# Hash attention with a gated MLP: stripes of hash results with gaps, gated rows kept in PSUM, and the last output row in three column parts

## The chip, the core and the metric

The kernel runs on one core of a Trainium2 chip. [...] VectorE (DVE), ScalarE (ACT) and GpSimd (POOL) do the elementwise work, and SyncE (SP) issues most transfers. The time is the device time of one execution in microseconds; the comparison is by the median of several executions.

## The reference

Attention over hash buckets, and behind it a gated feed-forward network with a gated residual. Sizes: 4 batches, 8 heads, 768 positions, 64 values per head; 3072 tokens of 512 values; a hidden width of 1536. All inputs are fp32.

```python
q_bits = (einsum('bhsd,dk->bhsk', q, proj) > 0)          # 6 sign bits per position
k_bits = (einsum('bhsd,dk->bhsk', k, proj) > 0)
mask   = bucket(q_bits)[:, :, :, None] == bucket(k_bits)[:, :, None, :]
scores = where(mask, (q @ k.T) / sqrt(64), -1e9)
attn   = exp(scores - max(scores)); attn /= attn.sum(-1) + 1e-9
x      = (attn @ v), as 3072 x 512
out    = x + sigmoid(x @ w_res) * ((gelu(x @ w_gate) * (x @ w_val)) @ w_out)
```

## The kernel before

The 32 heads are taken as 16 pairs, four pairs to a batch. For every pair, q and k are loaded in fp32 (`load`), cast to bf16 into one of four buffers `nat` (`cast`, POOL), and extended by six columns that hold the hash bits as plus or minus one half, so that one product of 71 rows gives score and bucket comparison together. The extended rows are turned so that the feature runs over the partitions: in the first batch by PE (`turn_pe`, copied to `aug` by `turned` on DVE, L329), later by a transposing DMA (`turn`, L308, issued by SP).

The hash bits come about in four steps. `tr` (L240, DVE) transposes the loaded tile in blocks of 32 x 32; `hash_mm` (L251, PE) multiplies by the projection into a PSUM tile `hs`; `hash_tok` (L266, DVE) transposes this back into a tile of 12 stripes of 32 columns, which is the SBUF tile `ht` for pairs 1, 2 and 3 and the PSUM tile `htp` for all later pairs; `bits` (L282) compares with zero and writes the six columns, in four instructions of 32 partitions by 12 rows by 6 values. For the first batch's q all four are DVE's, for its k POOL and DVE take turns. Pair 0 has its own path (`hash_one`, `bits_one`).

Each pair has nine chunks. `scores` (L448, PE) fills a PSUM tile of 128 x 1024 (`sp`, two of them), ACT takes the exponential (L459), `values` (L421, PE) multiplies by v into accumulators `av`, and `finish` divides (L372 and L373, DVE). POOL prepares v: `vals_a` (L338) and `vals_s` (L346 to L350). In the first batch the order of all steps is written out by hand in the list `ORDER`; each engine runs its instructions in that order. The weights of the network are loaded by POOL in twelve pieces (`w0` to `w11` in the lists, L193).

When a batch's attention is done, `gate_val` (L472 PE, L489 ACT, L492 DVE) computes the hidden layer in twelve blocks; beside the first batch's blocks stand the steps of the list `BESIDE` (loads, hashes and turns of the next pairs). Then `project` gives the output rows, six of 128 tokens per batch: four products `rps` for the residual gate (L504) with a tanh on ACT (L508), twelve products `fps` (L518), and on DVE two operations, L521 (gate plus one, times the product) and L524 (one half of that, plus x). SP sends the row out (L526). In the first three batches these products are spread over the next batch's chunks, and `rps` and `fps` alternate between two PSUM banks; the last batch's six rows run one behind the other at the end, with `fps` in the two `sp` tiles.

The function `project` splits the very last row by columns:

```python
for k0, k1 in ((0, 3), (3, 4)) if last else ((0, KM),):
    cs = slice(k0 * P, k1 * P)
```

Of the kernel before, what the change touches and what calls it, by code (L numbers as in the profile page):

```python
# [9 lines left out]
FP32 = mybir.dt.float32  # L10
# [36 lines left out]
def kernel(  # L47
# [12 lines left out]
    nc = tc.nc  # L60
    B, H, S, D = q.shape
    NBITS = proj.shape[1]
    DMODEL = H * D
    DFF = moe_w_gate.shape[1]
    P = 128
    KM = DMODEL // P
# [4 lines left out]
    HT = 2 * T  # L71
# [22 lines left out]
    sm_pool = ctx.enter_context(tc.tile_pool(name="sm", bufs=2))  # L94
    sc_ps = ctx.enter_context(tc.tile_pool(name="sc_ps", bufs=2, space=PSUM))
    av_ps = ctx.enter_context(tc.tile_pool(name="av_ps", bufs=2, space=PSUM))
# [5 lines left out]
    x_tok, x_sb = {}, {}  # L102
# [79 lines left out]
    for s in range(NS):  # L182
        cs = bass.ts(s, DFF // NS)
# [3 lines left out]
    for s in range(3):  # L187
        n = KF // 3
# [8 lines left out]
    def nat_of(x):  # L197
        return nat[(2 * x[0] + x[1]) % NN]
# [13 lines left out]
    t32, hsum, htok = {}, {}, {}  # L212
    free_banks, held_banks = ["r", "f"], {}

    def take(what=None):
        tag = free_banks.pop(0)
        if what is None:
            free_banks.append(tag)
        else:
            held_banks[what] = tag  # L220
        return tag

    def give(what):
        if what in held_banks:
            free_banks.append(held_banks.pop(what))
# [31 lines left out]
    def ht_of(jobs):  # L257
        return jobs[0]

    def hash_tok(jobs, psum=False):  # L260
        n = 32 * len(jobs)
        if psum:
            ht = mm_ps.tile([P, HT, 32], FP32, tag=take(("ht", ht_of(jobs))), name="htp")
        else:
            ht = sm_pool.tile([P, HT, 32], FP32, tag="ht", name="ht")
        nc.vector.transpose(ht[:n].rearrange("p c n -> p (c n)"),  # L266
                            hsum[jobs[0]][:n].rearrange("p c n -> p (c n)"))
        give(jobs[0])
        for j, x in enumerate(jobs):
            htok[x] = (ht, j)  # L270
        ht_left[id(ht)] = (len(jobs), ("ht", ht_of(jobs)))

    def bits(p, side, engs=(nc.vector,)):
        x = (p, side)
        ht, j = htok.pop(x)
        n, what = ht_left.pop(id(ht))
        if n > 1:
            ht_left[id(ht)] = (n - 1, what)
        else:
            give(what)  # L280
        for a in range(4):
            engs[a % len(engs)].tensor_scalar(  # L282
                nat_of(x)[32 * a:32 * a + 32, :, D:D + NBITS],
                ht[32 * j:32 * j + 32, :, NBITS * a:NBITS * (a + 1)], 0.0, 0.5,
                op0=ALU.is_gt, op1=ALU.subtract)


# [73 lines left out]
    av = {}  # L361
# [136 lines left out]
    def project(b):  # L498
        hh = hidden[b]
        for t in range(T):  # L500
            last = b == B - 1 and t == T - 1
            rps = mm_ps.tile([P, DMODEL], FP32, tag=take(), name="rps")
            for kk in range(KM):
                nc.tensor.matmul(rps, x_sb[b][:, kk, t, :], wr[:, kk, :],  # L504
                                 start=(kk == 0), stop=(kk == KM - 1))
                if kk == KM - 1:
                    th = g_pool.tile([P, DMODEL], FP32, tag="th", name="th")
                    nc.scalar.activation(th, rps, AF.Tanh, scale=0.5)  # L508
                yield
            o = o_pool.tile([P, DMODEL], FP32, tag="o", name="o")  # L510
            for k0, k1 in ((0, 3), (3, 4)) if last else ((0, KM),):
                cs = slice(k0 * P, k1 * P)
                if b < B - 1:
                    fps = mm_ps.tile([P, DMODEL], FP32, tag=take(), name="fps")
                else:
                    fps = sc_ps.tile([P, DMODEL], FP32, tag="sp", name="fps")
                for m in range(KF):
                    nc.tensor.matmul(fps[:, cs], hh[:, m, bass.ts(t, P)], wo[:, m, cs],  # L518
                                     start=(m == 0), stop=(m == KF - 1))
                    yield  # L520
                nc.vector.scalar_tensor_tensor(o[:, cs], th[:, cs], 1.0, fps[:, cs],  # L521
                                               op0=ALU.add, op1=ALU.mult)
                o3 = o[:, cs].rearrange("p (k n) -> p k n", n=P)
                nc.vector.scalar_tensor_tensor(o3, o3, 0.5, x_tok[b][:, k0:k1, t, :],  # L524
                                               op0=ALU.mult, op1=ALU.add)
                nc.sync.dma_start(out_t[b, t][:, cs], o[:, cs])  # L526

# [63 lines left out]
    def tokens(ps, psum=False):  # L591
        hash_tok([(p, side) for p in ps for side in range(2)], psum)
# [6 lines left out]
    def hash_pe(ps, s, bits_at):  # L599
        jobs = [(p, side) for p in ps for side in range(2)]  # L600
        for i in range(4):
            pe(s + i // 2 - 1, lambda i=i: hash_mm(jobs, (i % 2,), (i // 2,)))
        at(s, lambda: tokens(ps))
        for p, s in zip(ps, bits_at):
            at(s, lambda p=p: bits(p, 0), lambda p=p: bits(p, 1, (nc.gpsimd, nc.vector)))
# [30 lines left out]
    for p in range(1, 2 * HP):  # L636
        for side in range(2):
            job(f"tr{p}{side}", lambda p=p, side=side: tr(p, side))
            job(f"cs{p}{side}", lambda p=p, side=side: cast(p, side, nc.gpsimd))
            job(f"bt{p}{side}", lambda p=p, side=side: bits(p, side, (nc.vector,) if side == 0 or p >= HP else (nc.gpsimd, nc.vector)))  # L640
            job(f"tu{p}{side}", lambda p=p, side=side: turn(p, side))
            for hi in range(2):
                job(f"tp{p}{side}{hi}", lambda p=p, side=side, hi=hi: turn_pe(p, side, hi))
                job(f"td{p}{side}{hi}", lambda p=p, side=side, hi=hi: turned(p, side, hi, nc.vector))
# [21 lines left out]
    def lay(b, m, x):  # L666
        gv(b, m, lambda: bits(*x), lambda: turn(*x))
# [45 lines left out]

    gate_val(0, begun)
    mlp.append(project(0))
    for s in range(NSLOT, LAST):
        p, c = divmod(s, NCH)
        b, slot = divmod(s, NSLOT)
        cur = scores(p, c)
        for piece in side_pe.pop(s, []):  # L720
            piece()
        mlp_mm(AHEAD + (slot + 1) * (NMM - HELD - AHEAD) // NSLOT - done[0])
        pending.append(cur)
        while len(pending) > LAG:
            values(*pending.pop(0))
        for piece in side_work.pop(s, []):
            piece()
        if slot == NSLOT - 1:
            values(*pending.pop(0))
            ps = (HP * (b + 1), HP * (b + 1) + 1)  # L730
            mlp_mm(4)
            flush()
            begun = [gv_mm(b, 0, w, 0, KM - 1) for w in (wg, wv)]
            if b < B - 1:
                mlp_mm(NMM)
                gate_val(b, begun, lambda: hashed(ps))
            else:
                x_turn(b, HP - 1)
                mlp_mm(HELD - 7)
                gv(b, 0, lambda: mlp_mm(NMM))  # L740
                gate_val(b, begun, lambda: mlp_mm(3))
            done[0] = 0
            mlp.append(project(b))
# [33 lines left out]
```

## Time and profile before

| | |
|---|---|
| median of 3 executions | 346.66 us (346.12 to 347.13) |
| profiled execution | 346.07 us, its span 344.4 us |
| PE | 333.5 us busy, 97% of the span |
| ACT | 206.2 us, 60% |
| DVE | 191.7 us, 56% |
| POOL | 85.6 us, 25% |
| moved by DMA | 42.90 MB |

The profile is one execution. A row of a timeline gives start, length, engine, line, operation, tiles, shapes and count; behind it, in square brackets, stands how long the engine was idle before it and what ended that. Rows of neighbouring instructions of one kind are merged, so a row with x2 covers two instructions and what lies between them. A group row gives minimum, median and maximum of one instruction in ns.

### The profile page before, as it was taken

The page shows a single profiled execution, that of the slowest core. Times are in us where ns is not written, and L with a number is a line of the kernel's source. Part 1 is how long each engine was busy: PE and PEld are TensorE (multiplying, and loading weights), DVE is VectorE, ACT ScalarE, POOL GpSimd, SP SyncE. Part 2 cuts the span into 40 slices and gives each one's busy share as a digit, 9 for nine tenths or more (in the row PEclk, how much of TensorE's full clock was granted, in tenths as well). Part 3 has the DMA queues.
Part 4 walks back from the last instruction along what each step waited for, and adds up shares of the span by engine and source line. Part 5 has one row for each costly group of instructions (what it writes and reads, how often), then busy time and mean ns, then how long its engine had stood idle before and what let it go on. Part 6 is the DMA issues. An engine that isn't in the chain of part 4 may idle for free.

```text
span 344.4 us, 7546 instructions
## 1 busy us (share of the span) xinstructions
PE 333.5 (97%) x3064; PEld 204.3 (59%) x3112; DVE 191.7 (56%) x404; ACT 206.2 (60%) x232; POOL 85.6 (25%) x162
## 2 busy tenths in 40 slices
PE   8998999999999999999999999999999999999994
PEld 4675766555666655655666665656566665566442
DVE  6979737656344856757344784747244444343333
ACT  3888972226999962224999982223999984223110
POOL 3887920317055000260043200242030000000000
PEclk9999999999999999999999999999999999999999
DMA  7959998999976743528366642725430220000022
GB/s 215 376 128 280 146 241 149 181 127 176 189 175 188 210 107 78 101 39 148 82 194 188 227 115 65 131 49 109 75 100 32 55 55 30 33 0 0 32 79 75
DMA packets 71171, 42.90 MB, mean 125 GB/s; under 512 B 49504, under 2 KB 68192, under 8 KB 71136
## 3 DMA queue, kind: packets, MB, share of 16 engines
q1 hardware_dynamic: 64720, 37.17, 44.0%
q0 software_dynamic: 6336, 5.24, 10.2%
q8 instruction: 24, 0.39, 0.5%
q14 instruction: 11, 0.09, 0.1%
q10 hardware_dynamic: 80, 0.00, 0.0%
HBM read 29.36 MB, written 6.29 MB: 104 GB/s over the span
## 4 chain that ended last, share of the span: by engine, by line
PE 90%; DVE 3%; ACT 3%; issue 1%; DMA 1%; SPq 0%; POOL 0%; DVEq 0%; ACTq 0%; POOLq 0%
PE sp L472 34%; PE fps L518 18%; PE sp L448 17%; PE av L421 9%; PE rps L504 6%; PE hs L251 3%; ACT hh L459 2%; DMA ld<-in_k_dram 1%; PE pt L320 1%; PE wps L174 1%; DVE nat L282 1%; PE hs L293 1%; DVE aug L329 1%; ACT gt L489 0%; SPq L308 0%
## 5 line engine op out<-in xcount | busy, mean ns | idle before, releaser
L459 ACT ACTIVATE e<-sp 128x1024 bf16<-128x1024 f32 x108 | 109.0, 1028 | 8.0 <-PE sp L448 2.8
L489 ACT ACTIVATE gt<-sp 128x768 bf16<-128x768 f32 x48 | 38.9, 810 | 92.8 <-PE sp L472 92.8
L448 PE MATMUL sp<-aug,aug 71*128 71x256 bf16 (+1 forms) x384 | 85.8, 325 | 2.0 <-DVE aug L329 1.6
L518 PE MATMUL fps<-wo,hh 128*128 128x512 bf16 (+2 forms) x275 | 74.6, 369 | 1.4
L492 DVE TENSOR_TENSOR hh<-gt,sp 128x768 bf16<-128x768 bf16 x48 | 45.7, 953 | 48.0 <-PE sp L472 43.9
L472 PE MATMUL sp<-x_sb,wv 128*128 128x256 bf16 (+1 forms) x378 | 70.6, 325 | 0.7 <-DVE hh L492 0.4
L472 PE MATMUL sp<-x_sb,wg 128*128 128x256 bf16 (+1 forms) x373 | 70.4, 324 | 0.7
L421 PEld LDWEIGHTS <-e 128*128 128x128 bf16 x864 | 40.2, 97 | 25.1
L472 PEld LDWEIGHTS <-wv 128*128 128x128 bf16 x384 | 37.6, 98 | 25.3 <-issue 0.6
L472 PEld LDWEIGHTS <-wg 128*128 128x128 bf16 x384 | 36.7, 98 | 26.0 <-issue 2.3
L421 PE MATMUL av<-va,e 128*128 128x65 bf16 x864 | 43.4, 193 | 0.0
L518 PEld LDWEIGHTS <-hh 128*128 128x128 bf16 x300 | 27.4, 97 | 22.5
L459 ACT ACTIVATE hh<-sp 128x1024 bf16<-128x1024 f32 x36 | 34.4, 1026 | 5.1 <-PE sp L448 5.0
L521 DVE SCALAR_TENSOR_TENSOR o<-th,fps 128x512 f32<-128x512 f32 (+2 forms) x25 | 16.7, 666 | 36.9 <-PE fps L518 30.0
L448 PEld LDWEIGHTS <-aug 71*128 71x128 bf16 x384 | 29.2, 97 | 13.0 <-issue 2.0
L346 POOL TENSOR_TENSOR v<-ldv 128x384 f32<-128x384 f32 x16 | 16.0, 999 | 64.1 <-DMA ldv<-in_v_dram 64.0
L240 DVE STREAM_TRANSPOSE t<-ld 128x768 f32<-128x768 f32 (+1 forms) x34 | 30.5, 912 | 1.6 <-DMA ld<-in_k_dram 1.4
L400 DVE COPY av<-av 128x390 f32<-128x390 f32 x24 | 13.6, 567 | 29.7 <-PE av L396 29.7
L208 POOL TENSOR_SCALAR nat<-ld 128x768 bf16<-128x768 f32 (+1 forms) x16 | 13.8, 860 | 60.1 <-DMA aug<-nat 55.4
L504 PE MATMUL rps<-wr,x_sb 128*128 128x512 bf16 x90 | 25.6, 378 | 0.3
L508 ACT ACTIVATE th<-rps 128x512 f32<-128x512 f32 x24 | 14.3, 594 | 18.5 <-PE rps L504 18.5
L210 POOL CAST nat<-ld 128x768 bf16<-128x768 f32 (+1 forms) x17 | 13.3, 783 | 39.7 <-DMA aug<-nat 38.8
(64 smaller groups left out, 242.5 us busy)
## 6 DMA issues: line engine op xcount, KB each, us to landing
ldv<-in_v_dram SPq DMA_DIRECT2D x16, 384.0 KB, 5.4
out_dram<-o SPq DMA_DIRECT2D x23, 256.0 KB, 2.0
ld<-in_q_dram SPq DMA_DIRECT2D x15, 384.0 KB, 5.6
ld<-in_k_dram SPq DMA_DIRECT2D x15, 384.0 KB, 5.2
wg<-in_moe_w_gate_dram POOLq DMA_DIRECT2D x4, 384.0 KB, 8.5
wv<-in_moe_w_val_dram POOLq DMA_DIRECT2D x4, 384.0 KB, 9.0
wo<-in_moe_w_out_dram POOLq DMA_DIRECT2D x3, 512.0 KB, 9.4
wr<-in_moe_w_res_dram POOLq DMA_DIRECT2D x1, 512.0 KB, 7.7
```

The costliest lines, as they stand in the source:

```text
L240: nc.vector.transpose(t32[p, side][:, sl].rearrange("p c h n -> p (c h n)"), raw[p, side][:, sl].rearrange("p c d -> p (c d)"))
L346: nc.gpsimd.tensor_add(v3, vs[:, :, 0:3, :], vs[:, :, 3:6, :])
L421: nc.tensor.matmul(av[p, hi][:, qt, :], e[:, off:off + P], va[:, hi, jt, 0:D + 1], start=first, stop=(p >= HP and jt == T - 1), skip_group ...
L448: nc.tensor.matmul(sp[:, off:off + nq * P], ks[0:KA, hi * T + jt, :], qs[0:KA, hi * T + qt0:hi * T + qt0 + nq, :], start=True, stop=True)
L459: nc.scalar.activation(e, sp, AF.Exp, scale=float(ALPHA))
L472: nc.tensor.matmul(sp[:, c0:c1], w[:, kk, bass.ts(m, P)], xs[:, kk, c0:c1], start=(kk == 0), stop=(kk == KM - 1))
L489: nc.scalar.activation(gt, sp[:, 0:S], AF.Gelu)
L492: nc.vector.tensor_mul(hidden[b][:, m, :], gt, ps[1][:, 0:S])
L504: nc.tensor.matmul(rps, x_sb[b][:, kk, t, :], wr[:, kk, :], start=(kk == 0), stop=(kk == KM - 1))
L508: nc.scalar.activation(th, rps, AF.Tanh, scale=0.5)
L518: nc.tensor.matmul(fps[:, cs], hh[:, m, bass.ts(t, P)], wo[:, m, cs], start=(m == 0), stop=(m == KF - 1))
L521: nc.vector.scalar_tensor_tensor(o[:, cs], th[:, cs], 1.0, fps[:, cs], op0=ALU.add, op1=ALU.mult)
```

## The change

Three edits. First, the SBUF tile `ht` gets 15 stripes in place of 12, and the results are written and read as three groups of four with an empty stripe behind each; the PSUM tile `htp` keeps its 12. The instructions and their order stay, only their access patterns differ. Second, L521 writes its result over the product in its PSUM bank, in place of the SBUF tile `o`, and L524 reads it from there and writes `o`. Third, the last row has three column parts of 256, 128 and 128 columns in place of two of 384 and 128, the last of them in a bank of the pool that held the attention's accumulators; this adds twelve products with their weight loads, two DVE operations and one output transfer.

```diff
+    def stripes(ht):
+        n = ht.shape[1]
+        return ht.rearrange("p (a c) n -> p a c n", a=3)[:, :, 0:HT // 3] if n > HT else \
+            ht.rearrange("p (a c) n -> p a c n", a=3)
+
     def hash_tok(jobs, psum=False):
...
-            ht = sm_pool.tile([P, HT, 32], FP32, tag="ht", name="ht")
-        nc.vector.transpose(ht[:n].rearrange("p c n -> p (c n)"),
-                            hsum[jobs[0]][:n].rearrange("p c n -> p (c n)"))
+            ht = sm_pool.tile([P, HT + 3, 32], FP32, tag="ht", name="ht")
+        nc.vector.transpose(stripes(ht[:n]).rearrange("p a c n -> p a (c n)"),
+                            hsum[jobs[0]][:n].rearrange("p (a c) n -> p a (c n)", a=3))
...
             engs[a % len(engs)].tensor_scalar(
-                nat_of(x)[32 * a:32 * a + 32, :, D:D + NBITS],
-                ht[32 * j:32 * j + 32, :, NBITS * a:NBITS * (a + 1)], 0.0, 0.5,
+                nat_of(x)[32 * a:32 * a + 32, :, D:D + NBITS].rearrange("p (a c) n -> p a c n", a=3),
+                stripes(ht[32 * j:32 * j + 32, :, NBITS * a:NBITS * (a + 1)]), 0.0, 0.5,
                 op0=ALU.is_gt, op1=ALU.subtract)
...
-            for k0, k1 in ((0, 3), (3, 4)) if last else ((0, KM),):
+            for k0, k1 in ((0, 2), (2, 3), (3, 4)) if last else ((0, KM),):
                 cs = slice(k0 * P, k1 * P)
-                if b < B - 1:
+                if last and k1 == KM:
+                    fps = av_ps.tile([P, DMODEL], FP32, tag="av", name="fps")
+                elif b < B - 1:
...
-                nc.vector.scalar_tensor_tensor(o[:, cs], th[:, cs], 1.0, fps[:, cs],
+                nc.vector.scalar_tensor_tensor(fps[:, cs], th[:, cs], 1.0, fps[:, cs],
                                                op0=ALU.add, op1=ALU.mult)
                 o3 = o[:, cs].rearrange("p (k n) -> p k n", n=P)
-                nc.vector.scalar_tensor_tensor(o3, o3, 0.5, x_tok[b][:, k0:k1, t, :],
+                g3 = fps[:, cs].rearrange("p (k n) -> p k n", n=P)
+                nc.vector.scalar_tensor_tensor(o3, g3, 0.5, x_tok[b][:, k0:k1, t, :],
                                                op0=ALU.mult, op1=ALU.add)
```

## The prediction

> **What bounds the kernel now.** I read the page first (busy shares, chain), then the stage table, then the engines' timelines wherever an engine that should be full had a hole.
>
> ```profile
> PE 333.5 (97%) x3064; PEld 204.3 (59%) x3112; DVE 191.7 (56%) x404; ACT 206.2 (60%) x232; POOL 85.6 (25%) x162
> PE 90%; DVE 3%; ACT 3%; issue 1%; DMA 1%; SPq 0%; POOL 0%; DVEq 0%; ACTq 0%; POOLq 0%
> ```
>
> PE is busy for 97% of the span and carries 90% of the chain. The change leaves PE's columns as they are, so it can only win where PE stands still. One such place lies in the first batch, another is the tail behind the last product. The stage table (length; then busy us with counts of PE, PEld, DVE, ACT, POOL; clock; DMA share; GB/s) shows the first:
>
> ```profile
> 28.00:33.30 5.30, 3.87 (x50) 2.58 (x48) 5.14 (x11) 4.41 (x5) 5.13 (x10) 1.00 1.01 269
> 33.30:46.90 13.60, 13.37 (x209) 10.12 (x210) 9.81 (x18) 13.12 (x14) 11.56 (x19) 1.00 1.28 191
> 46.90:83.00 36.10, 35.34 (x268) 21.06 (x272) 22.64 (x53) 12.46 (x17) 10.32 (x16) 1.00 1.02 158
> ```
>
> From 28.0 to 33.3 us DVE is busy for 5.14 of 5.30 and PE for only 3.87. PE and ACT are nearly full afterwards. The timelines of PE, ACT and DVE around it:
>
> ```profile
> 31.72 0.38 PE L448 MATMUL sp<-aug,aug 71*128 71x256 bf16 x2
> 33.30 0.39 PE L448 MATMUL sp<-aug,aug 71*128 71x512 bf16 x1 [1.20 <-DVE aug L329]
> ```
> ```profile
> 15.21 5.83 ACT L459 ACTIVATE hh<-sp 128x1024 bf16<-128x1024 f32 x6 [0.29 <-PE sp L448]
> 21.45 1.94 ACT L459 ACTIVATE hh<-sp 128x1024 bf16<-128x1024 f32 x2 [0.41 <-PE sp L448]
> 23.86 8.55 ACT L459 ACTIVATE hh<-sp 128x1024 bf16<-128x1024 f32 x9 [0.47 <-PE sp L448]
> 33.78 1.02 ACT L459 ACTIVATE hh<-sp 128x1024 bf16<-128x1024 f32 x1 [1.37 <-PE sp L448]
> ```
> ```profile
> 28.07 0.90 DVE L282 TENSOR_SCALAR nat<-ht 32x72 bf16<-32x72 f32 x2
> 28.99 0.98 DVE L240 STREAM_TRANSPOSE t<-ld 128x768 f32<-128x768 f32 x1
> 29.98 2.21 DVE L282 TENSOR_SCALAR nat<-ht 32x72 bf16<-32x72 f32 x4
> 32.22 1.02 DVE L329 COPY aug<-pt 71x768 bf16<-71x768 bf16 x2
> ```
>
> The reader should see one wait on three engines: PE cannot finish a score tile until two copies of turned operands are done (32.22 to 33.24), ACT waits 1.37 us for that tile, and the copies are late because six bit writes (L282) in front of them took 3.11 us. Elsewhere the same write is short:
>
> ```profile
> L282 DVE TENSOR_SCALAR nat<-htp x96: 214/228/239, 53.3 to 241.3; 32x72 bf16<-32x72 f32 x96
> L282 DVE TENSOR_SCALAR nat<-ht x18: 185/194/1061, 15.6 to 31.1; 32x72 bf16<-32x72 f32 x18
> L282 POOL TENSOR_SCALAR nat<-ht x6: 448/468/513, 15.7 to 25.7; 32x72 bf16<-32x72 f32 x6
> ```
>
> Read from PSUM (htp) it never takes over 239 ns; read from SBUF (ht) its median is shorter, 194, but it can take 1061. The long ones, one by one, and what POOL does then:
>
> ```profile
> 28.07 0.69 DVE L282 TENSOR_SCALAR nat<-ht 32x72 bf16<-32x72 f32 x1
> 31.13 1.06 DVE L282 TENSOR_SCALAR nat<-ht 32x72 bf16<-32x72 f32 x1
> ```
> ```profile
> 27.81 0.82 POOL L338 CAST va<-ldv 128x768 bf16<-128x768 f32 x1 [1.70 <-DMA ldv<-in_v_dram]
> ```
> ```profile
> 28.62 0.98 POOL L193 DMA_DIRECT2D wg<-in_moe_w_gate_dram  x1
> 29.60 0.75 POOL L193 DMA_DIRECT2D wv<-in_moe_w_val_dram  x1
> 30.34 0.75 POOL L193 DMA_DIRECT2D wg<-in_moe_w_gate_dram  x1
> 31.10 1.02 POOL L346 TENSOR_TENSOR v<-ldv 128x384 f32<-128x384 f32 x1
> ```
>
> The write of 28.07 ends at 28.76, just behind POOL's cast (28.63); that of 31.13 ends at 32.19, just behind POOL's sum (32.12). The transpose of 28.99 ran through POOL's next two instructions in 0.98 us. So it is this form of write, and not DVE as a whole, that POOL holds up.
>
> **The gaps in the hash results.** In the built program the bit write's source becomes 3 groups of 4 stripes, while its destination stays 12 rows of 6. [...] No row shows such a source, so the write lies between no gain (it is still held) and the PSUM row's 228 ns. I take 228, since that is the same operation in the form that is never held. [...]
>
> Six writes at 0.228 make 1.37 in place of 3.11 us: DVE is 1.74 us earlier and the copies end at 31.50 in place of 33.24. What is late next is PE itself: its first part of that tile starts at 31.72 and the rest would follow at about 32.1, so PE's hole of 1.20 closes and no more. ACT's earlier block ends at 23.86 + 8.55 = 32.41; the tile used to reach it 0.48 after PE's restart, which gives 32.4 to 32.6. **Gain 1.20**, between 0 and ACT's 1.37.
>
> The other twelve writes were not held, and grow by 0.034 each: six in a row, 0.2 us, at 15.58 and at 23.90. Behind both lie blocks in which ACT has six and nine tiles without a hole (the rows of 15.21 and 23.86), so PE is ahead there. Zero to 0.2 each; I take 0.05 in all. If that cover were gone it would be 0.4. The two transposes into the striped tile write the same 384 elements per partition: nothing. The six POOL writes also get the third level: shown only as 0.468 us without it. POOL's 768-element cast of 0.82 bounds them above (two in a row, 0.7 later, with ACT's block behind), and DVE's 0.228 below. I take no change.
>
> **What follows the hole.** A stage that starts 1.2 us earlier meets the DMA engines as they were; their share is 1.28 and then 1.02 in the table. One wait there is already for a load:
>
> ```profile
> 62.10 0.98 DVE L240 STREAM_TRANSPOSE t<-ld 128x768 f32<-128x768 f32 x1 [1.36 <-DMA ld<-in_k_dram]
> ```
>
> That load is issued by SP behind turned operands, which come from DVE and move with it, while POOL's weight loads hardly move since POOL is full (5.13 of 5.30). If the load keeps its place, all of the gain is given back; if it moves along, none. I take 0.15 lost.
>
> **Gated rows over their bank.** The second operation reads PSUM in place of a second SBUF tile, and the first writes PSUM. The tail has both kinds at equal sizes:
>
> ```profile
> 337.25 0.69 DVE L524 SCALAR_TENSOR_TENSOR o<-o,x_tok 128x512 f32<-128x512 f32 x1
> 339.34 0.56 DVE L521 SCALAR_TENSOR_TENSOR o<-th,fps 128x384 f32<-128x384 f32 x1 [1.40 <-PE fps L518]
> 339.93 0.56 DVE L524 SCALAR_TENSOR_TENSOR o<-o,x_tok 128x384 f32<-128x384 f32 x1
> 340.41 0.28 DVE L521 SCALAR_TENSOR_TENSOR o<-th,fps 128x128 f32<-128x128 f32 x1
> 340.72 0.29 DVE L524 SCALAR_TENSOR_TENSOR o<-o,x_tok 128x128 f32<-128x128 f32 x1
> ```
>
> L521 reads PSUM and L524 does not, and they take 0.56 and 0.56, 0.28 and 0.29. So a PSUM source costs nothing; a PSUM target is not shown at this shape, and I take nothing. [...]
>
> The bank is now held until the second operation ends. The tightest place in the first three batches is this one:
>
> ```profile
> 116.78 0.69 DVE L524 SCALAR_TENSOR_TENSOR o<-o,x_tok 128x512 f32<-128x512 f32 x1
> ```
> ```profile
> 117.67 0.38 PE L518 MATMUL fps<-wo,hh 128*128 128x512 bf16 x1
> ```
>
> The second operation ends at 117.47 and PE returns to the bank at 117.67: 0.20 us are left. Free, as long as L524 does not grow. Only x_tok is then read from SBUF, and the wait for an old output's DMA moves from the first operation to the second; both are off the path.
>
> **The last row in three parts.** 256 + 128 + 128 columns in place of 384 + 128:
>
> ```profile
> 337.14 2.78 PE L518 MATMUL fps<-wo,hh 128*128 128x384 bf16 x24
> ```
> ```profile
> 337.30 1.96 PE fps L518 x12
> ```
>
> Twelve products of 384 columns end at 339.26, the twelve of 128 at 339.92, 0.055 each, so a column costs the same in both. Twelve more weight loads ride beside them. The parts then end at about 338.6, 339.26 and 339.92. DVE is free from 337.94. With 0.42 for 256 columns (halfway between 0.28 and 0.56), DVE runs 338.7 to 339.57, 339.5 to 340.10 and 340.02 to 340.62, where it ended at 341.01 before. **Gain 0.39**; PE's end plus 0.08, 0.28 and 0.29 and their gaps, 340.60, is the floor. The third bank comes from a pool that is empty by then; the second part's bank is that of row 4 and is free at 337.94. SP has one more output to issue, over 0.5 us ahead of the last, which stays 64 KB. Range 0.1 to 0.41; I take 0.35.
>
> **Sum.** −1.20 + 0.05 + 0.15 − 0.35 = −1.35. The profiled execution took 346.07 us (344.4 of span and 1.67 around it), 0.59 below the median of 346.66; it would take 344.7 with the change, and I take the same difference from the median: **345.3 us**.
>
> **Rivals.** *The early gain is eaten by the DMA* (load of 62.10 lands when it did): against it, SP's part moves with DVE; for it, the shares above 1. Only the tail and some 0.3 us remain: 346.0. *The gaps change nothing*: the write is still held, since no row shows the new source. [...] Against: 96 writes of one form without one long one. Only the tail: 346.3. *PE waits for its banks, and it is slower*: if reading PSUM beside an SBUF tile made the second operation longer by d, each of 18 rows in three batches could wait up to d − 0.20. It decides from d = 0.28 (18 × 0.08 = 1.4), an operation of 0.97 in place of 0.69; at d = 0.4 it costs up to 3.6 less 1.4, 348.9. The L521 rows, which do just such a read at 0.56, speak against it.
>
> **Numbers.** Forecast 0.62, DMA 0.15, no release 0.14, banks 0.09. The forecast's own range is 344.9 (both gains at their bounds, 1.37 and 0.41) to 345.6. Some 0.3% (1.04 us) is what a measurement of this kernel tells from no change, as its three runs lie 1.01 us apart. The first case is faster by more than that, the two middle ones within it, the last slower. The range of 344.5 to 346.5 takes in the first three, with 0.4 below the best case for the spread of the median.
>
> **What would show it.** Right: no bit write above 0.25 us, PE's 1.20 and ACT's 1.37 near 32 us gone, the wait at about 61 us still below 1.5, DVE's last operation 0.35 sooner behind the last row's first product. Wrong: long bit writes at POOL's ends, bit writes still at 194 ns, the wait for the load grown by 1.2, or PE waiting for DVE ahead of L518's line.

## The result, and the profile after

The changed kernel takes 344.12 us (median of 4, 343.89 to 344.56), the kernel before 346.45 us (median of 4; three of the four are those behind the 346.66 above). The ratio is 0.9932, with a 95% interval of 0.9913 to 0.9951. The forecast was 345.3, with a range of 344.5 to 346.5. So the direction was right and the gain larger than forecast: 2.33 us in place of 1.35, and 0.4 us below the range. The profiled execution took 344.56 us with a span of 342.9, which is 1.5 us less than the profiled execution before.

From the page of the changed kernel, the busy shares and the chain:

```profile
PE 333.6 (97%) x3076; PEld 205.3 (60%) x3124; DVE 190.3 (56%) x406; ACT 206.3 (60%) x232; POOL 84.1 (25%) x162
PE 91%; ACT 4%; issue 1%; DMA 1%; DVE 1%; SPq 0%; POOL 0%; DVEq 0%; POOLq 0%
```

The work of PE (TensorE, the engine of the MATMUL rows) is what it was (333.6 us busy); DVE's share of the chain fell from 3% to 1%. The table of the same three stretches of the changed kernel:

```profile
28.00:33.30 5.30, 5.07 (x73) 3.65 (x70) 4.91 (x12) 5.30 (x6) 5.13 (x9) 1.00 1.02 268
33.30:46.90 13.60, 13.37 (x204) 10.02 (x203) 8.77 (x18) 13.58 (x15) 11.72 (x21) 1.00 1.29 196
46.90:83.00 36.10, 35.16 (x259) 20.68 (x263) 23.29 (x54) 12.35 (x17) 11.12 (x19) 1.00 1.07 162
```

From 28.0 to 33.3 us PE is busy for 5.07 us where it was 3.87, and ACT is full. The DMA shares (1.02, 1.29, 1.07) are nearly those of before. The hole is closed on PE, ACT and DVE, as their timelines show:

```profile
31.93 0.60 PE L453 MATMUL sp<-aug,aug 71*128 71x256 bf16 x3
```
```profile
21.66 1.94 ACT L464 ACTIVATE hh<-sp 128x1024 bf16<-128x1024 f32 x2 [0.42 <-PE sp L453]
24.07 21.71 ACT L464 ACTIVATE hh<-sp 128x1024 bf16<-128x1024 f32 x23 [0.47 <-PE sp L453]
```
```profile
28.29 0.46 DVE L287 TENSOR_SCALAR nat<-ht 32x72 bf16<-32x72 f32 x2
28.76 0.98 DVE L240 STREAM_TRANSPOSE t<-ld 128x768 f32<-128x768 f32 x1
29.75 0.91 DVE L287 TENSOR_SCALAR nat<-ht 32x72 bf16<-32x72 f32 x4
30.70 1.02 DVE L334 COPY aug<-pt 71x768 bf16<-71x768 bf16 x2
```

The six bit writes take 0.46 and 0.91 us where they took 0.90 and 2.21, and ACT runs 23 exponentials in one block where it stood still for 1.37 us after nine. POOL's instructions lie as before, in its timeline:

```profile
27.92 0.82 POOL L343 CAST va<-ldv 128x768 bf16<-128x768 f32 x1 [1.64 <-DMA ldv<-in_v_dram]
31.22 1.03 POOL L351 TENSOR_TENSOR v<-ldv 128x384 f32<-128x384 f32 x1
```

So the cast still runs beside the first two writes (28.29 to 28.75) and no longer holds them. The writes grouped by their source (minimum, median, maximum in ns):

```profile
L287 DVE TENSOR_SCALAR nat<-htp x96: 214/228/239, 52.1 to 240.3; 32x72 bf16<-32x72 f32 x96
L287 DVE TENSOR_SCALAR nat<-ht x18: 215/219/227, 15.8 to 30.4; 32x72 bf16<-32x72 f32 x18
L287 POOL TENSOR_SCALAR nat<-ht x6: 448/452/478, 15.9 to 25.8; 32x72 bf16<-32x72 f32 x6
```

The median write got 25 ns longer (194 to 219) and the longest fell from 1061 to 227 ns. The timeline of DVE at the end of the changed kernel, and its output transfers (KB each, median us from issue to landing):

```profile
337.69 0.43 DVE L528 SCALAR_TENSOR_TENSOR fps<-th,fps 128x256 f32<-128x256 f32 x1 [0.75 <-PE fps L525]
338.15 0.42 DVE L532 SCALAR_TENSOR_TENSOR o<-fps,x_tok 128x256 f32<-128x256 f32 x1
338.50 0.29 DVE L528 SCALAR_TENSOR_TENSOR fps<-th,fps 128x128 f32<-128x128 f32 x1
338.82 0.29 DVE L532 SCALAR_TENSOR_TENSOR o<-fps,x_tok 128x128 f32<-128x128 f32 x1
339.02 0.29 DVE L528 SCALAR_TENSOR_TENSOR fps<-th,fps 128x128 f32<-128x128 f32 x1
339.35 0.29 DVE L532 SCALAR_TENSOR_TENSOR o<-fps,x_tok 128x128 f32<-128x128 f32 x1
```
```profile
out_dram<-o SPq DMA_DIRECT2D x1, 128.0 KB, 1.7
out_dram<-o SPq DMA_DIRECT2D x2, 64.0 KB, 1.5
```

PE's timeline of the three parts shows when its last product ends:

```profile
336.11 2.81 PE L525 MATMUL fps<-wo,hh 128*128 128x256 bf16 x36
```

The second part's products end at 338.25 (worked out from the trace), while DVE is still at the first part until 338.57, so DVE works from 337.69 to its end at 339.64 almost without a pause. PE's last product ends at 338.92, and the last part's first operation starts 0.10 us later. The median of the two 64 KB transfers is 1.5 us from issue to landing; the one in the kernel before took 1.6:

```profile
out_dram<-o SPq DMA_DIRECT2D x1, 64.0 KB, 1.6
```

### The profile page after: what moved, and what is told of

It is laid out like the page before. It is cut to its first block, busy times and chain, and to the rows that moved or that the text cites. A ratio compares the mean times of both kernels' runs of the same rounds, so it can differ in the third digit from the quotient of the medians.

```text
span 342.9 us, 7598 instructions
## 1 busy us (share of the span) xinstructions
PE 333.6 (97%) x3076; PEld 205.3 (60%) x3124; DVE 190.3 (56%) x406; ACT 206.3 (60%) x232; POOL 84.1 (25%) x162
## 4 chain that ended last, share of the span: by engine, by line
PE 91%; ACT 4%; issue 1%; DMA 1%; DVE 1%; SPq 0%; POOL 0%; DVEq 0%; POOLq 0%
PE sp L477 34%; PE fps L525 17%; PE sp L453 17%; PE av L426 9%; PE rps L509 6%; ACT hh L464 3%; PE hs L251 3%; DMA ld<-in_k_dram 1%; PE pt L325 1%; PE wps L174 1%; PE hs L298 1%; ACT gt L494 0%; SPq L313 0%; PE pt L410 0%; DVE o L532 0%
## 5 line engine op out<-in xcount | busy, mean ns | idle before, releaser
L525 PEld LDWEIGHTS <-hh 128*128 128x128 bf16 x312 | 28.1, 97 | 21.8
L528 DVE SCALAR_TENSOR_TENSOR fps<-th,fps 128x512 f32<-128x512 f32 (+2 forms) x26 | 17.0, 654 | 36.1 <-PE fps L525 34.8
L208 POOL TENSOR_SCALAR nat<-ld 128x768 bf16<-128x768 f32 (+1 forms) x16 | 13.0, 813 | 59.8 <-DMA aug<-nat 56.3
L287 DVE TENSOR_SCALAR nat<-htp 32x72 bf16<-32x72 f32 x96 | 21.9, 229 | 1.8
```

The lines of the kernel that those rows point to most:

```text
L287: engs[a % len(engs)].tensor_scalar(nat_of(x)[32 * a:32 * a + 32, :, D:D + NBITS].rearrange("p (a c) n -> p a c n", a=3), stripes(ht[32 * ...
L528: nc.vector.scalar_tensor_tensor(fps[:, cs], th[:, cs], 1.0, fps[:, cs], op0=ALU.add, op1=ALU.mult)
```

## The experiments

Every kernel here computes the whole reference. A "session" is a set of runs on one chip with one shared median of the kernel before; each session had another chip.

**First session (before: 345.89, 30 runs): each edit alone, and another form of the gaps.**

`e1_gaps`: the gaps alone.

```diff
-            ht = sm_pool.tile([P, HT, 32], FP32, tag="ht", name="ht")
+            ht = sm_pool.tile([P, HT + 3, 32], FP32, tag="ht", name="ht")
...
-                ht[32 * j:32 * j + 32, :, NBITS * a:NBITS * (a + 1)], 0.0, 0.5,
+                stripes(ht[32 * j:32 * j + 32, :, NBITS * a:NBITS * (a + 1)]), 0.0, 0.5,
```

> Only the gaps in the SBUF hash results. Theory A (the prediction's sizes hold, the rest of the 2.3 us is spread between executions): 1.0 to 1.4 us faster than before. Theory B (the hole of the bit writes is larger in most executions than in the profiled one): 1.7 to 2.2 faster. Theory C (the in-place rows bring the rest): 1.0 to 1.4 faster here and the missing 0.8 in the run of the in-place rows alone. All: SBUF bit writes near 219 ns with none above 250, PE's hole of 1.20 us near 32 us at most 0.2.

344.69 us (median of 7), ratio 0.9969 (0.9956 to 0.9982): 1.20 us faster, what the forecast had for this part. The bit writes of this kernel, and ACT beside them:

```profile
L287 DVE TENSOR_SCALAR nat<-ht x18: 216/219/223, 15.4 to 30.1; 32x72 bf16<-32x72 f32 x18
```
```profile
23.72 21.71 ACT L464 ACTIVATE hh<-sp 128x1024 bf16<-128x1024 f32 x23 [0.47 <-PE sp L453]
```

`e2_inplace`: the gated rows over their bank, alone.

```diff
-                nc.vector.scalar_tensor_tensor(o[:, cs], th[:, cs], 1.0, fps[:, cs],
+                nc.vector.scalar_tensor_tensor(fps[:, cs], th[:, cs], 1.0, fps[:, cs],
...
-                nc.vector.scalar_tensor_tensor(o3, o3, 0.5, x_tok[b][:, k0:k1, t, :],
+                nc.vector.scalar_tensor_tensor(o3, g3, 0.5, x_tok[b][:, k0:k1, t, :],
```

> Only the gated rows written over their PSUM bank. Theories A and B: within 0.3 us of before, long bit writes still there. Theory C: 0.6 to 1.0 faster. The rival of the prediction (PE waits for banks): slower; not expected, since the changed kernel's product rows show no such wait.

345.88 us (12), ratio 0.9994 (0.9982 to 1.0005): nothing. Its profile shows the hole of the kernel before in another size. DVE and POOL of this kernel:

```profile
28.68 0.40 DVE L282 TENSOR_SCALAR nat<-ht 32x72 bf16<-32x72 f32 x2
30.09 2.01 DVE L282 TENSOR_SCALAR nat<-ht 32x72 bf16<-32x72 f32 x4
```
```profile
27.72 0.82 POOL L338 CAST va<-ldv 128x768 bf16<-128x768 f32 x1 [1.00 <-DMA ldv<-in_v_dram]
```

The cast was over at 28.54, before the first write at 28.68, and two writes took 0.40 in place of 0.90. The last two long writes were still held (0.50 and 1.05 us in the trace). What the hole costs thus depends on where POOL stands, and no edit of this kernel touches that.

`e3_parts`: the three column parts alone.

```diff
-            for k0, k1 in ((0, 3), (3, 4)) if last else ((0, KM),):
+            for k0, k1 in ((0, 2), (2, 3), (3, 4)) if last else ((0, KM),):
```

> Only the three column parts of the last row. All theories: 0.3 to 0.5 us faster than before, all of it between the last row's first product and the last DVE operation (3.87 us there before, 3.53 or less with three parts); long bit writes still there.

345.41 us (12), ratio 0.9983 (0.9973 to 0.9994): 0.48 us faster. The three separate medians add up to −1.20 − 0.01 − 0.48 = −1.69.

`e4_gaps2x6`: two groups of six stripes in place of three of four, with two empty stripes.

```diff
-            ht = sm_pool.tile([P, HT + 3, 32], FP32, tag="ht", name="ht")
+            ht = sm_pool.tile([P, HT + 2, 32], FP32, tag="ht", name="ht")
...
-                nat_of(x)[32 * a:32 * a + 32, :, D:D + NBITS].rearrange("p (a c) n -> p a c n", a=3),
+                nat_of(x)[32 * a:32 * a + 32, :, D:D + NBITS].rearrange("p (a c) n -> p a c n", a=2),
```

> Gaps too, but behind every sixth stripe: the source has 2 groups of 6, an even count, against 12 rows in the destination. [...] Rival (the spacing or the third level of the pattern itself frees the write): bit writes near 219 ns, none long, and the gain of the gaps by four.

345.66 us (11), ratio 1.0 (0.9988 to 1.0012): as before, within the 0.3 us forecast for the case that POOL still holds such a write. The bit writes and DVE's timeline of this kernel:

```profile
L287 DVE TENSOR_SCALAR nat<-ht x18: 185/194/1056, 15.1 to 30.5; 32x72 bf16<-32x72 f32 x18
```
```profile
29.22 2.30 DVE L287 TENSOR_SCALAR nat<-ht 32x72 bf16<-32x72 f32 x4
```

Gaps are there, and the write is as short (194) and as long (1056) as without them. So it is neither the gap itself nor the third level of the pattern that takes the write out of the form that POOL holds. What differs is three groups of four against two of six. Why that decides is not shown; no other count of groups was tried.

**Second session (before: 346.47, 17 runs): the whole again, one edit left out, the kernel before against itself, and POOL moved.**

`e5_all` is the changed kernel again.

> The changed kernel once more, in as many rounds as its parts. If the parts simply add (gaps 1.1, three parts 0.5, rows in place 0.0, by their medians) it is 1.4 to 1.9 us faster than before, and the 2.3 of the first result was mostly the draw of its few executions. If the parts help each other beyond their sum: 2.1 or more faster.

344.10 us (6), ratio 0.9940 (0.9924 to 0.9955): 2.37 us faster, as the second of the two theories had it. The third session did not repeat it.

`e6_gaps_parts` has the gaps and the parts; the rows stay in SBUF.

```diff
-                nc.vector.scalar_tensor_tensor(fps[:, cs], th[:, cs], 1.0, fps[:, cs],
+                nc.vector.scalar_tensor_tensor(o[:, cs], th[:, cs], 1.0, fps[:, cs],
```

> Gaps and three parts, the gated rows in SBUF as before. If the rows in place bring nothing: within 0.3 us of the whole change. If they bring what the first result had beyond the forecast: 0.6 to 1.0 slower than the whole change.

344.95 us (6), ratio 0.9960 (0.9945 to 0.9976). That is 0.85 us above the whole change, which made the rows in place look useful; the third session did not repeat it.

`e7_null` is the kernel before, without an edit.

> The kernel before against itself. The ratio is 1.000 within 0.0012; its profile is one more draw of the start (first eight hash products, 1.5 to 2.6 us so far) and of the hole at the bit writes (PE waits 0.5 to 1.2 so far, larger where the first of the six writes meets POOL's cast).

346.24 us (12), ratio 0.9991 (0.9978 to 1.0004): two medians of one kernel differ by 0.23 us in one session.

`e8_pool_away` is the kernel before, without gaps, and with POOL's steps `va4`, `vs2`, `w0`, `w1` and `w2` moved behind `cs41` in `ORDER`, so that POOL stands idle beside the six writes.

```diff
-s17 ld51 va4 v14 s18 tr50 tp201 w0 w1 w2 bt30 td201 s19 v15 vs2 s20 tp211 cs41
+s17 ld51 v14 s18 tr50 tp201 bt30 td201 s19 v15 s20 tp211 cs41 va4 vs2 w0 w1 w2
```

> The kernel before, with no gaps, but POOL's cast, its weight loads and its sums queued behind a cast that waits for PE, so that POOL stands still while DVE writes the bits at 28 to 31 us. [...] Rival (the long writes come from the writes themselves, or from the DMA traffic then): long ones stay, no gain.

347.90 us (6), ratio 1.0051 (1.0032 to 1.0071), so it is slower as a whole, where 0.8 to 1.3 us faster was forecast, if POOL's later work is not late for PE. But the writes in question are short, near the forecast of 0.19 us each and none above 0.25. The group of bit writes, DVE and POOL of this kernel:

```profile
L282 DVE TENSOR_SCALAR nat<-ht x18: 186/191/282, 16.2 to 30.7; 32x72 bf16<-32x72 f32 x18
```
```profile
28.66 0.40 DVE L282 TENSOR_SCALAR nat<-ht 32x72 bf16<-32x72 f32 x2
30.07 0.80 DVE L282 TENSOR_SCALAR nat<-ht 32x72 bf16<-32x72 f32 x4
```
```profile
31.36 0.82 POOL L210 CAST nat<-ld 128x768 bf16<-128x768 f32 x1 [4.66 <-issue]
```

POOL does nothing for 4.66 us ahead of 31.36, the six writes of the unchanged form take 0.40 and 0.80, and the stage from the first to the last exponential of the first batch is 37.07 us, as with the gaps. This ties the long writes to POOL's work by a second way that leaves the write's form alone. The move also takes three weight loads out of that time, so this run alone does not part POOL's work from the transfers; but in `e2_inplace`, where the loads stood in their place, the first two writes were short as soon as the cast was over. The price came behind it: PE's timeline shows

```profile
47.54 0.81 PE L472 MATMUL sp<-x_sb,wg 128*128 128x512 bf16 x4 [1.50 <-DMA x_sb<-x_tok]
```

a wait of 1.50 us at the head of the gate products, and the middle of the kernel is 2.3 us longer. How POOL's delay reaches that transfer was not followed.

**Third session (before: 345.97, 21 runs): the pairs of edits, and the whole a third time.**

`e9_gaps_inplace` has the hunks of the first and the second diff above, without the third.

> Gaps and rows in place, the last row in two parts. If the rows in place bring nothing in company either: as the gaps alone, 0.9 to 1.4 us faster than before. If they bring 0.8 beside the gaps: 1.7 to 2.2 faster.

344.97 us (9), ratio 0.9964 (0.9948 to 0.9980): 1.00 us faster, as the gaps alone.

`e10_inplace_parts` has the second and the third.

> Rows in place and three parts, no gaps. If the rows in place bring nothing: as the three parts alone, 0.3 to 0.6 us faster than before. If they bring 0.8 beside the three parts: 1.1 to 1.5 faster.

345.98 us (12), ratio 0.9989 (0.9975 to 1.0003). The medians do not show the parts here, though the ratio would be 0.38 us and this kernel's profile has the shorter end (4.39 us in the table below); 0.4 us is near what such a comparison can tell.

`e11_all` is the changed kernel.

> The changed kernel a third time. By the stages of the profiles (1.2 at the bit writes, 0.4 behind the last row's first product, 0.1 behind the last DVE operation) 1.7 us faster than before; by the two results so far 2.3.

344.49 us (6), ratio 0.9949 (0.9931 to 0.9966): 1.48 us faster, nearer to the 1.7 of the stages.

`e12_gaps_parts` is the kernel of `e6_gaps_parts`.

> Gaps and three parts a second time, on the same chip as the changed kernel: within 0.3 us of it if the rows in place bring nothing, 0.6 to 1.0 slower if the difference of 0.85 between the two in their last runs was the rows'.

344.30 us (7), ratio 0.9952 (0.9935 to 0.9970). With and without the rows in place the time is the same here (344.49 and 344.30).

**Four single executions of the kernel before**, for a theory on the part of the gain that the stages do not hold: that the hole is longer in other executions than in the first profile.

> One more profiled execution of the kernel before. If the six profiles stand for the rest: 37.7 to 38.6 us from the first exponential's start to the last one's end, the first one starting at 7.9 to 9.2. If the missing 0.3 to 0.4 us lies in this stage: over 38.6 in most of the four looks.

> As the look before it: 37.7 to 38.6 us for the stage by the one, over 38.6 by the other.

> As the look before it: 37.7 to 38.6 us for the stage by the one, over 38.6 by the other.

> As the look before it: 37.7 to 38.6 us for the stage by the one, over 38.6 by the other.

345.73, 345.12, 345.43 and 346.44 us. The stage of the hole was 38.36, 38.04, 38.10 and 38.04 us, against 38.44 in the first profile. It is not longer, and the theory falls.

## Why the prediction was right in its mechanism and short in its size

A table over the profiles settles where the time went. Each is cut at the first exponential's start, the last exponential of the first batch, the start of the last row's `rps` products, and the end of DVE's last operation (us, worked out from the timelines):

| profiles | bit-write stage | middle | last row | behind DVE | sum |
|---|---|---|---|---|---|
| kernel before, mean of 6 (the first, `e7_null` and the four single ones) | 38.22 (38.04 to 38.44) | 289.49 | 4.74 | 3.34 | 335.79 |
| changed, mean of 3 | 37.06 (all three) | 289.43 | 4.39 | 3.20 | 334.08 |
| difference | −1.16 | −0.06 | −0.35 | −0.14 | −1.71 |
| in place (`e2_inplace`) | 37.73 | 289.32 | 4.77 | 3.31 | 335.12 |
| parts (`e3_parts`) | 38.57 | 289.50 | 4.36 | 3.21 | 335.64 |
| gaps (`e1_gaps`) | 37.06 | 289.48 | 4.74 | 3.31 | 334.59 |
| gaps, in place (`e9_gaps_inplace`) | 37.06 | 289.50 | 4.77 | 3.35 | 334.68 |
| gaps, parts (`e6_gaps_parts`) | 37.06 | 289.71 | 4.36 | 3.21 | 334.34 |
| gaps, parts (`e12_gaps_parts`) | 37.06 | 289.44 | 4.35 | 3.18 | 334.03 |
| in place, parts (`e10_inplace_parts`) | 38.29 | 289.43 | 4.39 | 3.18 | 335.29 |

**The gaps: right in the cause, and near in the size by luck.** The signs that the prediction named for being right came: no DVE bit write above 0.25 us, the holes of PE and ACT near 32 us gone, the wait at about 61 us at 1.49, and DVE's last operation 0.35 us sooner. That POOL holds up the old form of the write stands too. `e4_gaps2x6` and `e8_pool_away` each change one side of it: two groups leave the write at 194 ns and up to 1056 in POOL's way, and with POOL away the six writes of the old form take 188 to 195 ns. The last of the six took 1054 to 1062 ns in all ten profiles with the old form, or with two groups, and POOL in place; none of the 126 writes in the seven profiles with three groups took over 227. The prediction shows two long writes. The timeline of the kernel before has two more between them:

```profile
29.98 0.40 DVE L282 TENSOR_SCALAR nat<-ht 32x72 bf16<-32x72 f32 x1
30.60 0.52 DVE L282 TENSOR_SCALAR nat<-ht 32x72 bf16<-32x72 f32 x1
```

They end at 30.38 and 31.11, just behind the second and third of POOL's weight loads (30.35 and 31.09). So POOL's issuing of loads seems to hold writes too, and not only its cast and its sum; two others beside such loads, at 28.78 and 30.40, took no longer than 0.20 us, and why they ran free is open. The value taken for a write, 228, was 219. That three groups against twelve rows would not be held was the author's estimate; no run shows its cause. What the traces show is 2 groups against 12 rows at 185 ns at best and 194 in the median, and held up to 1056; 3 against 12 at 215 to 227, and never held.

The size was forecast as 1.20 us, PE's hole, because PE itself would be late next. It was not: with the gaps ACT runs on without a pause, and the stage is 37.06 us in every profile. What the gaps bring is thus ACT's whole hole. In the profile that the prediction read that is 38.44 − 37.06 = 1.38, the upper bound of its term (1.37). Over the six profiles of the kernel before it is 0.98 to 1.38, with a mean of 1.16, and in `e2_inplace` it was 0.67. That the 1.20 lies near the mean, and near the 1.20 between the medians of `e1_gaps`, is luck.

**The twelve other writes: +0.05 forecast, nothing came.** ACT's block of six after the first of them, in its timeline, is 5.82 us long in the changed kernel and was 5.83 before. POOL's six writes, taken as unchanged, have a median of 452 ns in place of 468.

**What follows the hole: 0.15 was taken as lost, and nothing was.** The load moved along. DVE's timeline of the changed kernel has

```profile
61.07 0.98 DVE L240 STREAM_TRANSPOSE t<-ld 128x768 f32<-128x768 f32 x1 [1.49 <-DMA ld<-in_k_dram]
```

1.03 us ahead of its place before (62.10), with a wait of 1.49 in place of 1.36; the middle as a whole is 289.43 against 289.49. The rival in which the DMA eats the gain is refuted, and so is the one in which the gaps change nothing.

**Rows in place: right, nothing.** `e2_inplace` is at 0.9994; `e9_gaps_inplace` is at 0.9964 where `e1_gaps` has 0.9969, `e11_all` at 0.9949 where `e12_gaps_parts` has 0.9952, each far inside the other's interval. The second operation did change, as a group of the kernel before and of the changed one shows (busy us, mean ns):

```profile
L524 DVE SCALAR_TENSOR_TENSOR o<-o,x_tok 128x512 f32<-128x512 f32 x23 | 16.4, 715 | 0.8
```
```profile
L532 DVE SCALAR_TENSOR_TENSOR o<-fps,x_tok 128x512 f32<-128x512 f32 x23 | 15.9, 691 | 0.8
```

It became 24 ns shorter on average, off the path, so the 0.28 us at which the slower rival begins never came near. The first operation, which now writes PSUM, went from 689 to 697 ns in the median of the full rows. Reading PSUM did not make the second operation longer: its full rows took 691 ns in the median with one input from PSUM, and 692 with both from SBUF before.

**The three parts: right in size where they were priced, short behind them.** Forecast 0.35, measured 0.35 to DVE's last operation. The time behind that operation was not in the sum, and it fell by another 0.14. In the traces of the two first profiles only 0.03 of that lies in the last transfer (1.56 to 1.53 us from issue to landing), and 0.10 between its landing and the end of the span (1.76 to 1.66). There SP waits for the transfers' semaphores one after another in a fixed order. The last output's semaphore comes one place later in this order with three parts than with two (in the fourth of ten waits in place of the third), so one wait fewer stands behind it. The profiles agree on the size (1.72 to 1.76 us in all with two parts, 1.62 to 1.66 in all with three); the order as its cause was not tested.

**The steps that failed.** The first is the limit behind the hole: "PE's hole of 1.20 closes and no more" was wrong, since all of ACT's hole closed. The number does not show it, because the hole that was read was the longest of six. In the sum, the +0.15 and the +0.05 did not come, and the time behind DVE, put at nothing because the last output stays 64 KB, fell by 0.14. By the stages the sum is −1.71 in place of −1.35. From the median of 346.66 that is 344.95, inside the range. The larger failure is the last step, "I take the same difference from the median", with "0.4 below the best case for the spread of the median". That median was a high draw: the medians of the kernel before were 346.66, 346.45, 345.89, 346.47 and 345.97, that is 0.77 apart, and the mean of 84 executions, the single ones left out, is 346.13. So of the 1.2 us between 345.3 and 344.12 the sum accounts for 0.36 and the base for 0.53. The other 0.3 is not assigned; 0.18 of it is how far the first four executions of the changed kernel lie below the mean of all its 16, 344.30. The medians of the changed kernel were 344.12, 344.10 and 344.49. The difference came out as 2.33, 2.37 and 1.48 in three comparisons; the forecast's ratio, 0.9961, lies outside the first two intervals and inside the third (0.9931 to 0.9966). A range for one such comparison needed about 0.8 for the medians, not 0.4.

**What stays open.** The mean of the three differences is 2.06, against 1.71 by the stages and 1.69 by the sum of the separate edits. The difference of the means over all executions, 346.13 − 344.30 = 1.83 with a 95% interval of 0.23 to either side, takes in 1.71, though it mixes chips in unequal shares. One part of the excess can be named, as an estimate: by their clocks, the runs of the kernel before in the second session started late (see the last section), which is worth some 0.3 us there. The time of every execution is 1.7 to 1.8 us above its span, so nothing is hidden outside the span. The hole's length is excluded as far as four executions can; nothing else was isolated.

## What to carry to other kernels

When short DVE instructions are long at some places only, lay their ends beside POOL's timeline: a form that is faster alone (194 ns) can be the slower one in company (up to 1061), and a change of the access pattern that costs 25 ns can be the cure. When a wait shows on several engines, price its end by the engine that runs on behind it (here ACT, 1.38), and over several profiles, since its length is a draw. Compare executions from a common event, such as the first exponential, rather than from the span's start; here that took a spread of 1.3 us out of a difference of 1.7. And take the base of a blind forecast with the spread of its medians between sessions, not within one.

## What the runs showed of the hardware

**The start of a run varies, whatever the kernel.** The first exponential starts between 7.92 and 9.20 us after the span's start, and this follows the first eight fp32 products. PE and ACT of `e5_all`, then of `e9_gaps_inplace`:

```profile
4.24 1.50 PE L298 MATMUL hs<-t,projs 128*128 128x192 f32 x8
```
```profile
8.08 1.02 ACT L464 ACTIVATE hh<-sp 128x1024 bf16<-128x1024 f32 x1 [1.04 <-PE sp L453]
```
```profile
4.24 2.63 PE L298 MATMUL hs<-t,projs 128*128 128x192 f32 x8
```
```profile
9.20 1.02 ACT L464 ACTIVATE hh<-sp 128x1024 bf16<-128x1024 f32 x1 [1.37 <-PE sp L453]
```

Eight equal products take 1.50 or 2.63 us, and all else follows 1.12 us later. The profile's row of the granted clock shows full speed there in both, but the clock records in the kept traces tell more. Each trace has one stretch at full speed, 337.92 us long in all 18, then one at half speed, and no record ahead of them; where there is none, the row reads as full speed. The stretch begins 4.30 us into the span in `e5_all`, as the eight products start, and 6.60 us in `e9_gaps_inplace`, near their end. Over the 18 profiles the first exponential starts at 6.14 us plus 0.46 times that moment, within 0.09 us (a fit). So each us of delay costs about half a us (0.46 in the fit). That TensorE ran at about half speed until then is an estimate from this figure and from the 2.63 us against 1.50; no record shows it.

A mean granted clock of 0.997 or 0.998 comes from what lies behind PE's work here. In the first profile of the kernel before (0.998), the half speed begins at 342.97 us, behind PE's last product (339.92), and the earlier the start, the sooner it begins. The moment can be estimated for other executions whose mean clock is below 1, as span − 337.92 − 2 × (1 − clock) × span. For the kernel before its mean is 5.1 and 5.0 us in the first and third sessions, 5.7 in the second, and 5.0 in `e7_null` (each clock is rounded to 0.001, 0.7 us).

**With two SBUF inputs, the second operation was longer beside POOL in three places.** The second operation of a full row took 715 ns on average and at most 916 in the kernel before, and at most 692 in the changed kernel, with one input from PSUM. Of the 23 in the kernel before, three took over 694 ns (803, 916 and 886), and all three ran beside POOL's casts and sums, at 99.2, 178.9 and 187.9 us; a fourth, beside sums at 108.1, took 694. In the changed kernel the four that ran beside POOL's casts and sums, at 98.2, 107.1, 177.9 and 186.9 us, took 691 or 692 like the others. Why, no trace shows.
